# A second buffer for streamed weight rows, v weights in pieces into their place, and statistics inside the folds

## The chip, the cores and the metric

The kernel runs on one core of one Trainium2 chip, as one launch. The metric is the time of an execution in device microseconds (us). The kernel before took 717.04 us (median of three runs, 717.01 to 718.02). A core has five engines that run side by side, each with its own queue of instructions in a fixed order: TensorE (PE) multiplies matrices, VectorE (DVE), ScalarE (ACT) and GpSimd (POOL) do elementwise work, and SyncE (SP) issues the transfers (DMAs) here. They wait for each other through semaphores.

## The reference

The input x has 2048 tokens of 640 channels. Everything is float32. Cut to what matters:

```python
xn = layernorm(x)
# A: linear attention, 32 heads of 20 channels
q, k, v = split(xn @ wqkv)                      # 640 x 1920
pq, pk = per_head(q @ w_phi), per_head(k @ w_phi)
phi = lambda p: concat(softmax(p), softmax(-p))
kv, z = phi(pk).T @ v, sum(phi(pk))
A = (phi(pq) @ kv / (phi(pq) @ z + 1e-6)) @ wo  # 640 x 640
# B: MLP with its own layernorm, 1728 hidden units
B = gelu(layernorm(xn) @ w1 + b1) @ w2 + b2
return x + A + B
```

## The kernel before, in words

**Split products.** Each float32 operand is split into a high part (a rounded copy, made by ACT) and a low part (the rest, made by DVE or POOL). A product is three matmuls: high by high, high by low, low by high (`mm3`, L62 to L64). So every weight and every activation costs an ACT copy and a DVE or POOL subtraction before PE can use it.

**Blocks and chunks.** The 2048 tokens are four blocks of 512. The hidden units are 14 chunks of 128 (the last has 64). The span has three parts. In the first, to some 218 us, PE runs the MLP of blocks 0 and 1, and beside it weights and inputs for the later parts are prepared. In the second the k, v and q projections and the attention sums are made, in the third the MLP of blocks 2 and 3, and the output. The change is in the first part.

**The first part.** After a start (tokens turned, first four chunks), `cycle(g)` for g = 2 to 5 handles chunks 2g and 2g+1 for both blocks with fewer products than four (sums and differences of the halves of weights and activations, `t1` to `t4`, are multiplied). Then `mlp.passes(6, b, ...)` does chunks 12 and 13 in the plain way, for block 0 and then 1: first layer, gelu, second layer. Results leave PE through eight PSUM banks: 0 to 2 for the first layer, 3 and 4 for the folds, 5 to 7 for the second layer. The second layer's bank is added to `acc` by DVE (L311) and then free for PE again.

**Steps.** The order on PE, DVE, ACT and POOL is written out by hand. Each time PE has been given one `mm3` in a place that allows it, `next(mlp.beside)` takes one step of the work beside: `at_steps` holds (step, action) pairs, and `both` runs two such lists in step. One cycle has 38 steps. The order on SP is not written out: a scheduler places its transfers. A step is a place in the order, not a time: an engine that must wait holds everything behind it.

**What runs beside.** `weight_events` makes the operands of the next cycle from two loaded tiles of w1 (ACT L501, POOL L504, POOL L507 for sums). `second_half(j)` splits 128 rows of w2 (ACT L501, POOL L504); they come through `load_second` (SP L556) into one buffer, `r2`, so that a load is issued when the split before has read it. `prep()` has one order: `folds` multiplies weights of q and k by the head's feature map on PE (L606) and splits and stores the results; `more_stats` takes the layernorm statistics of tokens 1024 to 2047 (L129), at two of every ten steps of the folds; then `rows` turns means and scales through PE, bank 3 or 4, and sends them through DRAM; then ten tiles of y for blocks 2 and 3 are made, eight steps each: subtract on POOL (L696), multiply on DVE (L699), high part on ACT (L703), low part on DVE (L706), two stores on SP (L708). Last, five tiles of v's weights are loaded into a staging tile (L668) and split into `wkv_`. The k part of `wkv_` (product of the folds) comes back from DRAM in two loads (L824).

**At the start** POOL makes two sums of 1024 columns for `traw` (L470), and `t_events` makes differences of them on DVE (L507).

Of the kernel before, what the change touches and what calls it, by code (L numbers as in the profile page):

```python
# [15 lines left out]
P = 128  # L16
# [27 lines left out]
def tile_kernel(ctx: ExitStack, tc: tile.TileContext, x, xT, wkT, wqT, wv, wphi, wo, w1, b1, w2, b2,  # L44
# [36 lines left out]
    wq_dram = [tc.dram_tile([P, KC, F1], F32, name=f"wq{p}") for p in "hl"]  # L81
    wk_dram = [tc.dram_tile([P, KC, F1], F32, name=f"wk{p}") for p in "hl"]
# [382 lines left out]
    def next_y():  # L465
# [3 lines left out]
        for i, c in ((0, slice(0, 2)), (3, slice(2, 4))):  # L469
            nc.gpsimd.tensor_tensor(q[i], f(h[:, c]), f(l[:, c]), op=ALU.add)  # L470
# [81 lines left out]
    r2 = [None]  # L552

    def load_second(c):
        r2[0] = rp.tile([P, D], F32, name="r2")
        nc.sync.dma_start(r2[0], w2[c * P:(c + 1) * P, :])  # L556

    load_second(4)
    mlp.beside = at_steps(*t_events(), *weight_events({"11": 10, "S1": 11, "12": 12, "15": 13, "s1": 14, "s2": 15, "S3": 16, "S4": 17,
# [105 lines left out]
    def prep():  # L665
        def load_v(kc):
            raw = fp.tile([P, D], F32, name="raw")
            nc.sync.dma_start(raw, wv[kc * P:(kc + 1) * P, :])  # L668
            return raw

        def load(b, c):
# [5 lines left out]
        loads = ahead([*(lambda job=job: raws(*job) for job in jobs), *(lambda job=job: load(*job) for job in todo),  # L677
                       *(lambda kc=kc: load_v(kc) for kc in range(KC))], 1)
# [46 lines left out]
    def cycle(g, other, side):  # L725
# [30 lines left out]
        def second_half(j):  # L756
            return [hi([x for x in (w2_[j][:, 0], w2_[j][:, 1])], r2[0]), lo([w2_[j][:, 0], w2_[j][:, 1]], r2[0], nc.gpsimd)]
# [4 lines left out]
                  (3, lambda: second_half(0)[0]()), (4, lambda: second_half(0)[1]()), (5, lambda: load_second(2 * g + 1)),  # L762
                  (12, lambda: second_half(1)[0]()), (13, lambda: second_half(1)[1]())]
        if g < 5:
            events += [(14, lambda: load_second(2 * g + 2)),
                       *weight_events({"11": 3, "S1": 4, "S3": 5, "s1": 7, "s2": 10, "S4": 11, "D5": 12, "12": 15, "15": 16, "s3": 18,
                                       "22": 22, "25": 23, "s4": 27, "d5": 28}, g + 2)]
        else:
            def take(c):
                def go():  # L770
                    mlp.raw[c] = araw[c - 12], rlast[c - 12]
# [4 lines left out]
            def load_last_seconds():  # L776
                load_second(12)
                rlast.append(r2[0])
                last = rp.tile([P, KC, P], F32, name="r1").rearrange("p a b -> p (a b)")
                for o in range(0, P, 64):  # L780
                    nc.sync.dma_start(last[o:o + 64, :], w2[13 * P:F, :])
                rlast.append(last)

            rlast = []
            mlp.spare = nc.gpsimd
            events += [(14, load_last_seconds), (16, take(12)), (19, take(13)), (27, lambda: ready[12][1][1]())]
# [31 lines left out]
    mlp.beside = side  # L818
# [733 lines left out]
```

## Time and profile before

The profiled execution took 717.25 us; its span from the first to the last instruction is 715.2 us.

| engine | busy us | share |
|---|---|---|
| PE (matmul) | 703.8 | 98% |
| DVE | 501.0 | 70% |
| POOL | 438.5 | 61% |
| ACT | 353.0 | 49% |

The DMA engines moved 103.41 MB, 145 GB/s in the mean. A row of the timeline gives the start and the duration in us, the engine, the line, the operation, output<-input by the program's names (buffer numbers left out, so `r2` reads `r`), the shape, and in brackets how long the engine had been idle before it and what ended the idle time. PE's matmuls overlap, so their durations are longer than the distance between their starts.

### The profile page before, as it was taken

The page shows a single profiled execution, that of the slowest core. Times are in us where ns is not written, and L with a number is a line of the kernel's source. Part 1 is how long each engine was busy: PE and PEld are TensorE (multiplying, and loading weights), DVE is VectorE, ACT ScalarE, POOL GpSimd, SP SyncE. Part 2 cuts the span into 40 slices and gives each one's busy share as a digit, 9 for nine tenths or more (in the row PEclk, how much of TensorE's full clock was granted, in tenths as well). Part 3 has the DMA queues.
Part 4 walks back from the last instruction along what each step waited for, and adds up shares of the span by engine and source line. Part 5 has one row for each costly group of instructions (what it writes and reads, how often), then busy time and mean ns, then how long its engine had stood idle before and what let it go on. Part 6 is the DMA issues. An engine that isn't in the chain of part 4 may idle for free.

```text
span 715.2 us, 9901 instructions
## 1 busy us (share of the span) xinstructions
PE 703.8 (98%) x3368; PEld 592.6 (83%) x3368; DVE 501.0 (70%) x837; ACT 353.0 (49%) x624; POOL 438.5 (61%) x408
## 2 busy tenths in 40 slices
PE   9999999999899999999999999999999999999998
PEld 7778888877778888888888888888888888888887
DVE  7886766496643788988978887845565646778753
ACT  7744546444343454454445447556565556551310
POOL 2584433666153797797787979655677777563400
PEclk9999999999999999999999999999999999999999
DMA  9516966455763224624600705674444753163222
GB/s 331 170 40 184 286 189 191 129 176 190 239 251 147 74 78 161 152 94 178 147 1 2 183 2 187 148 217 137 131 118 130 206 148 114 42 235 121 89 75 88
DMA packets 77047, 103.41 MB, mean 145 GB/s; under 512 B 22677, under 2 KB 45861, under 8 KB 75373
## 3 DMA queue, kind: packets, MB, share of 16 engines
q1 hardware_dynamic: 76996, 102.79, 46.0%
q8 instruction: 26, 0.43, 0.3%
q14 instruction: 25, 0.20, 0.1%
HBM read 69.79 MB, written 32.97 MB: 144 GB/s over the span
## 4 chain that ended last, share of the span: by engine, by line
PE 81%; DVE 6%; issue 4%; POOL 3%; DMA 3%; ACT 2%; SPq 0%; POOLq 0%; ACTq 0%; DVEq 0%
PE bank L62 24%; PE bank L63 24%; PE bank L64 24%; PE bank L943 3%; PE bank L606 2%; PE bank L1172 1%; PE bank L1171 1%; DVE q L507 1%; POOL w L504 1%; DMA yl<-raw 1%; DVE st L129 1%; DMA raw<-in_wv 1%; POOL raw L696 1%; DVE raw L706 1%; DVE acc L311 1%
## 5 line engine op out<-in xcount | busy, mean ns | idle before, releaser
L62 PE MATMUL bank<-m,w 128*128 128x512 f32 x266 | 106.5, 400 | 5.7 <-DVE acc L311 4.6
L62 PE MATMUL bank<-y,w 128*128 128x512 f32 (+1 forms) x270 | 104.7, 388 | 0.0
L64 PE MATMUL bank<-y,w 128*128 128x512 f32 (+1 forms) x270 | 104.3, 386 | 0.0
L63 PE MATMUL bank<-y,w 128*128 128x512 f32 (+1 forms) x270 | 104.2, 386 | 0.0
L64 PE MATMUL bank<-m,w 128*128 128x512 f32 x266 | 104.2, 392 | 0.0
L63 PE MATMUL bank<-m,w 128*128 128x512 f32 x262 | 102.7, 392 | 0.0
L311 DVE TENSOR_TENSOR acc<-bank,acc 128x512 f32<-128x512 f32 x120 | 80.7, 680 | 22.8 <-PE bank L64 18.4
L62 PE MATMUL bank<-wkh,y 128*128 128x512 f32 (+2 forms) x240 | 87.6, 365 | 0.0
L63 PE MATMUL bank<-wkl,y 128*128 128x512 f32 (+2 forms) x240 | 87.1, 363 | 0.0
L64 PE MATMUL bank<-wkh,y 128*128 128x512 f32 (+2 forms) x240 | 86.9, 362 | 0.0
L889 ACT ACTIVATE m<-bank 128x512 f32<-128x512 f32 (+1 forms) x64 | 26.5, 440 | 83.6 <-PE bank L64 60.2
L908 POOL TENSOR_TENSOR m<-m,mx 128x640 f32<-128x640 f32 (+2 forms) x48 | 44.4, 938 | 35.9 <-DVE mx L896 35.9
L62 PEld LDWEIGHTS bank<-m,w 128*128 128x128 f32 x266 | 50.3, 189 | 19.3 <-DVE acc L311 7.7
L1165 POOL TENSOR_TENSOR e<-e,m 128x512 fp32r<-128x512 f32 (+1 forms) x28 | 40.0, 1432 | 38.5 <-ACT m L1164 21.4
L64 PEld LDWEIGHTS bank<-y,w 128*128 128x128 f32 x270 | 50.7, 188 | 10.3
L64 PEld LDWEIGHTS bank<-m,w 128*128 128x128 f32 x266 | 50.3, 189 | 10.7
L62 PEld LDWEIGHTS bank<-y,w 128*128 128x128 f32 x270 | 50.7, 188 | 10.1
L63 PEld LDWEIGHTS bank<-y,w 128*128 128x128 f32 x270 | 50.7, 188 | 10.1
L915 DVE TENSOR_REDUCE sm<-m 128x64 f32<-128x1280 f32 x32 | 47.3, 1479 | 15.8 <-ACT m L913 15.6
L63 PEld LDWEIGHTS bank<-m,w 128*128 128x128 f32 x262 | 49.7, 190 | 9.7 <-DVE m L754 0.2
L913 ACT ACTIVATE m<-m,rs_all 128x1280 f32<-128x1280 f32 x32 | 43.8, 1368 | 21.8 <-POOL m L908 21.7
L56 POOL TENSOR_TENSOR w<-r,w 128x640 fp32r<-128x640 f32 x31 | 49.0, 1600 | 7.8 <-ACT w L53 7.7
(260 smaller groups left out, 1635.4 us busy)
## 6 DMA issues: line engine op xcount, KB each, us to landing
r<-in_w SPq DMA_DIRECT2D x43, 320.0 KB
e<-e SPq DMA_DIRECT2D x40, 256.0 KB
e<-acc SPq DMA_DIRECT2D x52, 160.0 KB
acc<-in_xT SPq DMA_DIRECT2D x4, 1280.0 KB
a<-in_w SPq DMA_DIRECT2D x9, 320.0 KB
xb<-in_x SPq DMA_DIRECT2D x8, 320.0 KB
xs<-in_x SPq DMA_DIRECT2D x8, 320.0 KB
raw<-in_xT SPq DMA_DIRECT2D x10, 256.0 KB
```

Of the source, the lines that this page charges most:

```text
L56: eng.tensor_tensor(lo, src, f(hi), op=ALU.subtract)
L62: nc.tensor.matmul(ps, lh, rh, start=first, stop=False, **kw)
L63: nc.tensor.matmul(ps, lh, rl, start=False, stop=False, **kw)
L64: nc.tensor.matmul(ps, ll, rh, start=False, stop=last, **kw)
L311: nc.vector.tensor_tensor(acc[b][:, m, :], pw, acc[b][:, m, :], op=ALU.add)
L606: nc.tensor.matmul(ps[:, c + i * kd:c + (i + 1) * kd], raw[n, g][:, (kc + i) * P:(kc + i + 1) * P], wpt[:, g, :kd // DF, 1:], start=True, ...
L889: return nc.scalar.activation(p3[:, :, c], ps.rearrange("p (h f) -> p h f", h=H), AF.Copy).ins
L908: subs[n, t] = nc.gpsimd.tensor_tensor(ep[:, s], a, b, op=ALU.subtract)
L913: exps[n, t] = nc.scalar.activation(e, e, AF.Exp, scale=rs_all[:, t:t + 1])
L915: nc.vector.tensor_reduce(sm, e.rearrange("p s (h f) -> p (s h) f", f=DH), axis=AX, op=ALU.add)
L943: nc.tensor.matmul(kvp[g // 2][:P, (g % 2) * 240:(g % 2) * 240 + 240].rearrange("p (s f) -> p s f", s=4), v[:, g * VS:g * VS + P], ft[:, : ...
L1165: nc.gpsimd.tensor_tensor(pl, e, f(ph), op=ALU.subtract)
```

## The change

- `load_second` gets two buffers, `r2` for even chunks and `r1` for odd ones, each loaded again after its own split has been read. Two loads are issued before the first cycle. Chunks 12 and 13 use the same two; the separate load of the last rows goes, and their split moves: chunk 12's from the last cycle into the last chunk pair, beside chunk 13's.
- v's weights are first copied inside DRAM to `wv_dram` (five transfers, at the beginning), then loaded in five pieces straight into the low part of `wkv_`, and split there in place, within `last_weights`; the staging loads at the end of `prep` go. The k weights come in ten pieces instead of two loads.
- The statistics are taken at three of every ten steps of the folds, and `rows` follows them there instead of after the folds. So the y tiles begin four steps earlier.
- POOL's two sums of 1024 columns become four of 512, and the first sum of weights (S1) moves from step 11 to 11.5.

```diff
-        for i, c in ((0, slice(0, 2)), (3, slice(2, 4))):
-            nc.gpsimd.tensor_tensor(q[i], f(h[:, c]), f(l[:, c]), op=ALU.add)
+        for c in range(4):
+            nc.gpsimd.tensor_tensor(q[c // 2 * 3][:, c % 2], f(h[:, c]), f(l[:, c]), op=ALU.add)
...
     def load_second(c):
-        r2[0] = rp.tile([P, D], F32, name="r2")
-        nc.sync.dma_start(r2[0], w2[c * P:(c + 1) * P, :])
+        r2[c % 2] = rp.tile([P, KC, P], F32, name=f"r{2 - c % 2}").rearrange("p a b -> p (a b)")
+        n = min(P, F - c * P)
+        for o in range(0, P, n):
+            nc.sync.dma_start(r2[c % 2][o:o + n, :], w2[c * P:c * P + n, :])
 
     load_second(4)
+    load_second(5)
+    copies = [(12 + 5 * kc, lambda kc=kc: nc.sync.dma_start(wv_dram[:, kc], wv[kc * P:(kc + 1) * P, :])) for kc in range(KC)]
...
-        loads = ahead([*(lambda job=job: raws(*job) for job in jobs), *(lambda job=job: load(*job) for job in todo),
-                       *(lambda kc=kc: load_v(kc) for kc in range(KC))], 1)
+        loads = ahead([*(lambda job=job: raws(*job) for job in jobs), *(lambda job=job: load(*job) for job in todo)], 1)
...
-        more = more_stats()
+        more = chain(more_stats(), rows(fp, mlp.px))
         for i, _ in enumerate(folds(loads)):
-            if i % 10 in (5, 8):
+            if i % 10 in (5, 7, 9):
                 next(more, None)
             yield
         fs.close()
         finish(more)
-        yield from rows(fp, mlp.px)
...
-        for kc in range(KC):
-            raw = next(loads)
-            for _ in range(3):
-                yield
-            split(*[w[:, kc, F1 + 2 * F2:] for w in wkv_], raw, eng=nc.gpsimd)
...
-                  (3, lambda: second_half(0)[0]()), (4, lambda: second_half(0)[1]()), (5, lambda: load_second(2 * g + 1)),
-                  (12, lambda: second_half(1)[0]()), (13, lambda: second_half(1)[1]())]
+                  (3, lambda: second_half(0)[0]()), (4, lambda: second_half(0)[1]()), (5, lambda: load_second(2 * g + 2)),
+                  (12, lambda: second_half(1)[0]()), (13, lambda: second_half(1)[1]()), (14, lambda: load_second(2 * g + 3))]
...
-            events += [(14, load_last_seconds), (16, take(12)), (19, take(13)), (27, lambda: ready[12][1][1]())]
+            events += [(16, take(12)), (19, take(13))]
...
-    for p in range(2):
-        nc.sync.dma_start(f(wkv_[p][:, :, :F1]), wk_dram[p])
+    def last_weights():
+        events = []
+        for kc in range(KC):
+            k, v = slice(0, F1), slice(F1 + 2 * F2, CB[2])
+            raw = f(wkv_[1][:, kc, v])
+            events += [(2 * kc, lambda kc=kc, raw=raw: nc.sync.dma_start(raw, wv_dram[:, kc])),
+                       (2 * kc + 7, lambda kc=kc, raw=raw: split(wkv_[0][:, kc, v], wkv_[1][:, kc, v], raw, eng=nc.gpsimd)),
+                       *((2 * kc + 10 + p, lambda kc=kc, p=p: nc.sync.dma_start(f(wkv_[p][:, kc, k]), wk_dram[p][:, kc])) for p in range(2))]
+        return at_steps(*events)
+    mlp.beside = both(last_weights(), side)
...
         if b == 0:
-            ready[13][1][1]()
+            for c in (12, 13):
+                ready[c][1][1]()
```

The diff tells little of where the scheduler puts SP's transfers, and of what stands behind what on POOL. On SP, at the end of the last cycle, before (`yh`, `yl` are y's stores, `raw<-in_xT` the loads of its tiles, `wkh` and `wkl` the two parts of `wkv_`, `in_wv` v's weights):

```order
L708 DMA yl_76<-raw 128x512
L673 DMA raw<-in_xT 128x512
L824 DMA wkh<-wkh 128x5x512
L824 DMA wkl<-wkl 128x5x512
L708 DMA yh_75<-xs 128x512
L708 DMA yl_76<-raw 128x512
```

and in the change, from the same store of y on:

```order
L706 DMA yl_76<-raw 128x512
L812 DMA wkl<-wv__79 128x640 x3
L673 DMA raw<-in_xT 128x512
L812 DMA wkl<-wv__79 128x640 x2
L814 DMA wkh<-wkh 128x512
L814 DMA wkl<-wkl 128x512
L814 DMA wkh<-wkh 128x512
L706 DMA yh_75<-xs 128x512
L814 DMA wkl<-wkl 128x512
L706 DMA yl_76<-raw 128x512
```

The v pieces now stand ahead of the k weights, and the last stores of y stand between the k pieces; before, v's loads came after them, at the end. On POOL, in the last chunk pair, before (`m<-m` of 64 rows is the low half of chunk 13's hidden units, L290, once for each block; `w` is the weight tile, `v` the tile of values):

```order
L290 TENSOR_TENSOR m_1948<-m_1921,m_1948 64x512
L243 MEMSET w_189 64x640
L244 TENSOR_TENSOR w_189<-r_1767,w_189 64x640
L56 TENSOR_TENSOR wkl<-raw,wkh 128x640 x3
L290 TENSOR_TENSOR m_2051<-m_2022,m_2051 64x512
L56 TENSOR_TENSOR wkl<-raw,wkh 128x640 x2
L861 MEMSET v_2165 128x1408
L861 MEMSET v_2168 128x1408
```

and in the change:

```order
L291 TENSOR_TENSOR m_1956<-m_1929,m_1956 64x512
L56 TENSOR_TENSOR w_189<-r_1735,w_189 128x640
L244 MEMSET w_190 64x640
L245 TENSOR_TENSOR w_190<-r_1783,w_190 64x640
L56 TENSOR_TENSOR wkl<-wkl,wkh 128x640 x4
L855 MEMSET v_2176 128x1408
L855 MEMSET v_2179 128x1408
L56 TENSOR_TENSOR wkl<-wkl,wkh 128x640
L291 TENSOR_TENSOR m_2066<-m_2038,m_2066 64x512
```

The second `m<-m` now stands behind all five splits of v, the split of chunk 12's rows of w2 and the two memsets; before, only three splits stood ahead of it.

More of the change, by code (lines that the diff above doesn't have):

```diff
@@ L1 @@
 from contextlib import ExitStack
-from itertools import zip_longest
+from itertools import chain, zip_longest
 import concourse.bass as bass
@@ L665, in prep @@
     def prep():
[L666 to L669, printed above, removed]
         def load(b, c):
@@ L756, in second_half @@
         def second_half(j):
-            return [hi([x for x in (w2_[j][:, 0], w2_[j][:, 1])], r2[0]), lo([w2_[j][:, 0], w2_[j][:, 1]], r2[0], nc.gpsimd)]
+            t = [w2_[j][:, 0], w2_[j][:, 1]]
+            return [hi(t, r2[j]), lo(t, r2[j], nc.gpsimd)]
         events = [(2, copy(za, "a")), (9, copy(zb, "a")), (14, total(za, "c")), (16, copy(zc, "a")), (16.5, total(zc, "d")),
@@ L770, in go @@
                 def go():
-                    mlp.raw[c] = araw[c - 12], rlast[c - 12]
+                    mlp.raw[c] = araw[c - 12], r2[c - 12]
                     ready[c] = mlp.take_parts(c, mlp.tiles[c % 4])
@@ L774, in take @@
                 return go
[L776 to L784, printed above, removed]
             mlp.spare = nc.gpsimd
-            events += [(14, load_last_seconds), (16, take(12)), (19, take(13)), (27, lambda: ready[12][1][1]())]
+            events += [(16, take(12)), (19, take(13))]
         mlp.beside = both(at_steps(*((when - 1, what) for when, what in events)), side)
```

11 lines of the change are left out of this document (5 added, 6 removed).

## The prediction

> **What bounds the kernel now.** I read the busy time of each engine first, then TensorE (PE) in stretches, then PE's rows at each place where its pace breaks, and last, for each such place, the rows of the engine that PE waited for.
>
> ```profile
> PE 703.8 (98%) x3368; PEld 592.6 (83%) x3368; DVE 501.0 (70%) x837; ACT 353.0 (49%) x624; POOL 438.5 (61%) x408
> ```
>
> PE is busy for 98% of the span, so a change that removes no matmul can win only the places where PE stands. The next view gives PE busy by stretch, with granted clock, DMA share and GB/s in the last three columns.
>
> ```profile
> 180.00:190.00 10.00, 8.77 (x32) 7.12 (x33) 7.44 (x12) 2.51 (x4) 0.03 (x1) 0.83 0.86 296
> 260.00:460.00 200.00, 200.00 (x1048) 174.98 (x1047) 168.30 (x253) 104.75 (x160) 166.15 (x167) 1.00 0.38 110
> ```
>
> From 260 to 460 PE never stands; in the ten microseconds after 180 it does. PE's own rows (start, duration, what; in brackets the idle time) show each place:
>
> ```profile
> 34.52 0.49 PE L62 MATMUL bank<-m,w 128*128 128x512 f32 x1 [1.04 <-DVE acc L309]
> 47.65 0.50 PE L62 MATMUL bank<-m,w 128*128 128x512 f32 x1 [0.35 <-DVE acc L311]
> 151.03 0.50 PE L62 MATMUL bank<-m,w 128*128 128x512 f32 x1 [0.31 <-DVE acc L311]
> 169.15 0.50 PE L62 MATMUL bank<-th,w 128*128 128x512 f32 x1 [0.95 <-ACT m L740]
> 178.45 0.39 PE L63 MATMUL bank<-m,w 128*128 128x512 f32 x1
> 178.68 0.39 PE L64 MATMUL bank<-m,w 128*128 128x512 f32 x1
> 181.23 0.80 PE L62 MATMUL bank<-m,w 128*128 128x512 f32 x1 [2.16 <-DVE acc L311]
> 184.70 0.39 PE L64 MATMUL bank<-m,w 128*128 128x512 f32 x1
> 187.00 0.39 PE L62 MATMUL bank<-y,w 128*128 128x512 f32 x1
> 210.44 0.50 PE L62 MATMUL bank<-m,w 128*128 128x512 f32 x1 [1.74 <-DVE acc L311]
> 213.52 0.39 PE L306 MATMUL bank<-m,w 128*128 128x512 f32 x1
> 218.50 0.39 PE L62 MATMUL bank<-wkh,y 128*128 128x512 f32 x1
> ```
>
> A matmul of 512 columns lasts 0.39 us but the next starts 0.23 us after it (178.45 to 178.68), so each bracketed idle time costs 0.16 us more than it says. The losses are 1.2 (at 34.52), 0.5 (47.65), 0.5 (151.03), 1.1 (169.15, call it A), 2.3 (181.23, call it B) and 1.9 us (210.44, call it C). B has a second part: from 181.23 to 184.70 are eight starts in 3.47 us where 1.82 would do, at a granted clock of 0.83 over the stretch, so B costs 2.3 + 1.6 = 3.9. Together 9.1 us stand to be won, and nothing more without taking out matmuls.
>
> The Trainium skill ("TensorE: Matmul & The Clock Gate", section "What's actually happening") puts the slow state after an idle window of about 3.4 us; here the clock sank after an idle time of 2.16 us, and not after 1.74. By the page's number the 1.6 us would not hang on B's gap and B would be worth 2.3; I go by the rows.
>
> **The change part by part.** A. The buffer for rows of w2 is single: on the queue of SyncE (SP) its load stands behind y's stores, and ScalarE (ACT) waits for it.
>
> ```profile
> 163.12 0.41 SPq L556 DMA_DIRECT2D r<-in_w  x1
> 167.36 0.74 ACT L501 ACTIVATE w<-r 128x640 fp32r<-128x640 f32 x1 [4.58 <-DMA r<-in_w]
> 168.52 0.58 ACT L740 ACTIVATE m<-bank 128x512 f32<-128x512 f32 x1
> 168.17 1.54 POOL L504 TENSOR_TENSOR w<-r,w 128x640 fp32r<-128x640 f32 x1 [6.25 <-ACT w L501]
> ```
>
> ACT stands 4.58 us at L501, the bank copy L740 queues behind it, and PE behind L740. With two buffers this load is issued a cycle earlier (some 26 us), as soon as GpSimd (POOL) has read the buffer's former rows. That removes all of A, 1.1 us. What is late next on ACT is nothing: the other operand of L740 is PE's own bank.
>
> B. The same wait holds POOL idle for 6.25 us, and the work that it should have done then collides with VectorE (DVE) later:
>
> ```profile
> 173.44 1.35 DVE L699 TENSOR_TENSOR raw<-raw,t 128x512 f32<-128x512 f32 x1 [1.19 <-POOL raw L696]
> 176.83 2.06 DVE L706 TENSOR_TENSOR raw<-raw,xs 128x512 fp32r<-128x512 f32 x1
> 179.42 1.16 DVE L699 TENSOR_TENSOR raw<-raw,t 128x512 f32<-128x512 f32 x1
> 182.29 0.68 DVE L706 TENSOR_TENSOR raw<-raw,xs 128x512 fp32r<-128x512 f32 x1
> 180.50 1.27 DVE L311 TENSOR_TENSOR acc<-bank,acc 128x512 f32<-128x512 f32 x2
> 176.32 2.02 POOL L56 TENSOR_TENSOR w<-r,w 128x640 fp32r<-128x640 f32 x1
> ```
>
> DVE stands 1.19 us for POOL, then L699, L706 and L699 take 1.35, 2.06 and 1.16 while POOL works, against 0.68 when it doesn't: 1.19 + 0.67 + 1.38 + 0.48 = 3.7 us of delay in front of the L311 that frees PE's bank. I follow the new order with these durations: the split of chunk 11 runs on POOL at some 163 instead of 168.2, one split (2.02 us) leaves this stretch for the next stage, and the y preparation starts four steps earlier, which puts L706 where L699 was. Then POOL is up to date at 171 and each L311 is done over 1 us before PE asks for its bank again. I take all of B, 3.9; the bounds are 0 (the collisions only move) and 3.9. The same shift is what I expect at 151.03: 0.5, bounds 0 and 0.5.
>
> C. The v weights' load blocks ACT (6.45 us), and with it the gelu on which DVE's L311 hangs.
>
> ```profile
> 206.25 0.74 ACT L53 ACTIVATE wkh<-raw 128x640 fp32r<-128x640 f32 x1 [6.45 <-DMA raw<-in_wv]
> 195.73 1.29 POOL L290 TENSOR_TENSOR m<-m,m 64x512 fp32r<-64x512 f32 x1 [3.73 <-issue]
> 196.97 0.63 POOL L243 MEMSET w<- 64x640 f32 x1
> 197.68 1.58 POOL L244 TENSOR_TENSOR w<-r,w 64x640 fp32r<-64x640 f32 x1
> 199.22 3.08 POOL L56 TENSOR_TENSOR wkl<-raw,wkh 128x640 fp32r<-128x640 f32 x2
> 215.74 2.49 POOL L861 MEMSET v<- 128x1408 f32 x2
> ```
>
> Now five pieces go straight into wkl, once PE and POOL have left that space (some 170 to 173), and land by about 178, well before ACT's first split. C as such is gone: 1.9. But it gives some back. Count from the start of the last chunk pair, t0 = 187.00 before. POOL's first L290 starts at t0 + 8.73. Behind it now stand, in one row, w2's split for chunk 12 (1.55, as L504 above), the memset (0.63) and L244 (1.58), four v splits (4 x 1.54), the two memsets of v (2.49, in front now, behind before), the fifth split (1.54) and only then the second L290 (1.29). Sum: 8.73 + 1.29 + 1.55 + 0.63 + 1.58 + 6.16 + 2.49 + 1.54 + 1.29 = 25.26; less 0.06 us of overlap at each border, some 24.9. PE, without C, comes to the L306 that reads this result at 213.52 - 187.00 - 1.9 = t0 + 24.6, and needs it a signal earlier. I take a new wait of 0.7 us (bounds 0 and 1.9). So C brings 1.2.
>
> Start. POOL's two sums of 1024 columns become four of 512, and the first sum of weights (S1) is put behind the first low half.
>
> ```profile
> 27.11 5.21 POOL L470 TENSOR_TENSOR q<-y,y 128x1024 f32<-128x1024 f32 x2
> 31.24 1.63 DVE L261 TENSOR_TENSOR m<-m,m 128x512 fp32r<-128x512 f32 x1
> 39.59 3.98 DVE L507 TENSOR_TENSOR q<-q,q 128x1024 f32<-128x1024 f32 x2 [1.63 <-POOL q L178]
> 40.77 1.73 POOL L507 TENSOR_TENSOR sraw<-a 128x256 f32<-128x256 f32 x1
> 46.92 0.68 DVE L311 TENSOR_TENSOR acc<-bank,acc 128x512 f32<-128x512 f32 x1
> ```
>
> L261 ends (32.87) half a microsecond after POOL's second sum (32.32): it waited for that instruction to end. With pieces of 1.3 us it ends some 1.3 us sooner, which pays the 1.2 at 34.52. PE then comes earlier to 47.65, but DVE there is set by POOL's chain (L507 starts when POOL's last sum is there), which the pieces don't shorten. What shortens it is S1: at 40.77 it collides with the second L507, and now waits for ACT. I take 0.6 to 0.9 off the L311 at 46.92, so the two stalls together bring 0.8 (bounds 0 and 1.7).
>
> Costs that I set near nothing. Two rows, the statistics of one tile's halves and the copy of the turned rows:
>
> ```profile
> L129 DVE BATCH_NORM_STATS2 st<-xs x16: 441/476/484, 70.8 to 100.0; 128x6 f32<-128x320 f32 x16
> 129.63 0.28 DVE L191 COPY sr<-bank 16x128 f32<-16x128 f32 x1
> ```
>
> The statistics come three to ten steps instead of two, one tile (2 x 0.48 and a small aggregate, 1.1 us) more in each of the first periods of ten steps (each step three matmuls, 0.68 us, and the folds' own); DVE has that room there, since the dense run of L311 comes only after step 28, where statistics stood before and stand no more. The turn of the rows through PE takes bank 3 one step before a fold uses it; the copy that frees it (0.28) stands behind one add of 0.68, so PE may wait 0 to 0.7; I take 0.15. The five copies of v inside DRAM (1.6 MB) are issued behind the last large load:
>
> ```profile
> 8.00:12.00 4.00, 3.97 (x30) 3.41 (x29) 3.79 (x15) 3.83 (x9) 1.56 (x1) 1.00 1.04 406
> 24.00:28.00 4.00, 4.00 (x21) 3.32 (x20) 2.00 (x9) 3.84 (x7) 1.03 (x2) 1.00 0.72 192
> ```
>
> The DMA engines are full at first (share 1.04) and done within the stretch that ends at 28 (0.72). At 390 GB/s the copies take 4.2 us, and 8.4 if reading and writing count apart; only the w1 rows of the next chunks stand behind them, due at 40.77 on POOL. Nothing is lost unless they take 14 us.
>
> Sum: 0.8 + 0.5 + 1.1 + 3.9 + 1.2 - 0.15 = 7.35; I keep 0.15 back for small waits not foreseen and say 7.2. The profiled execution took 717.25 us (span 715.2), 0.2 above the median 717.04; so 710.05 for an execution like it, **709.8 as a median**.
>
> **Rivals.** (1) B stays: DVE has as many instructions in that cycle as before, and the stretched ones may only meet POOL elsewhere. For it: DVE and POOL are 70% and 61% busy. Against it: POOL's 6.25 us of idle time are used. Then 717.04 - 7.2 + 3.9 = 713.7. (2) No wait comes in place of those removed, and the start brings everything: 717.04 - 9.1 = 707.9. Against it: the row of POOL work counted above. (3) Slower: the pieces don't overlap. Ten pieces of k (262 KB) and five of v (328 KB), 4.26 MB, stand where two loads of 1.3 MB stood, each needed whole at the projection, which comes at t0 + 31.5 less C, 209.9 on the new clock (t0 about 180.3). If each took the 4.2 us from issue to ACT's start that the load at 163.12 took, one behind the other, 15 pieces from 171 on would end at 234 and the projection would wait 24 us: 734. It decides at 4.26 MB in 39 us, 109 GB/s; below 92 the kernel is slower than before. Against it: the first loads, of 328 KB each, ran at 406 GB/s together. The Trainium skill ("DMA: Bandwidth & Descriptors", section "Measured (HBM→SBUF, 128 partitions, SWDGE, issued from GpSimd)") advises batches of at least 1 MiB, against this split; its fit of 2.0 us plus the bytes at 436 GB/s for each, one after another, would end at about 211 and cost some 1 us; it is measured on another queue than SP's, and the 406 GB/s here speaks against it. (4) The change doesn't do what it says: something else on the queues of ACT and SP holds the same stalls, within 1 us of before: 716.5.
>
> **How the numbers follow.** Forecast 0.61 (708.6 to 711.5 by its bounds on C and the start), (1) 0.15, (2) 0.11, (3) 0.05, (4) 0.08. A measurement of this kernel tells 0.2%, 1.4 us, from no change. Faster: 0.61 + 0.15 + 0.11 = 0.87; same 0.08; slower 0.05. The range runs from (2) to just past (1), 707.5 to 714.3.
>
> **What would show it.** Right: no idle time of ACT on loads of r or of v; PE without a gap from 120 to 200 and clock 1.00 in every slice; one gap of under a microsecond at the second L306 (now L307), released by POOL; the first gap near 34 gone and that near 47 longer. Wrong: a gap of over 1 us released by L311 in the cycle before the last chunk pair (then rival 1), a wait of PE for wkh or wkl at the first projection (rival 3), or a PE wait for a bank in the folds (then the statistics cost what I set at nothing).

## The result, and the profile after

The change takes 713.12 us (median of three runs, 712.67 to 713.58) against 717.04: the ratio is 0.9941, 95% interval 0.9918 to 0.9964. It is faster, by 3.9 us, and by 4.6 between the two profiled executions (717.25 to 712.67; spans 715.2 to 710.9). The prediction said 7.2 and 709.8. The time lies inside its range, next to the time of its first rival, but not for that rival's reason: what that rival expected to stay went away, and the missing 3 us lie elsewhere. Three profiled executions of the experiments below (`e3_y_later`, `e9_one_buffer_split_back` and `e11_before_split_late`) ran at a far lower pace throughout (spans of 1183.5, 1429.0 and 1429.0 us), so their gaps can't be read and they are left out of the times below.

The busy times of the change, and its window from 180 to 190 us (granted clock, DMA share and GB/s at the end):

```profile
PE 701.1 (99%) x3368; PEld 591.7 (83%) x3368; DVE 502.6 (71%) x837; ACT 353.0 (50%) x624; POOL 439.7 (62%) x410
```

```profile
180.00:190.00 10.00, 10.00 (x46) 8.28 (x45) 6.43 (x10) 3.18 (x5) 1.43 (x1) 1.00 1.03 393
```

In the stretch where PE was busy for 8.77 of 10 us at a clock of 0.83 it is now busy throughout at 1.00. PE's own rows in the change, at the places that the prediction named (each bracket again costs 0.16 us more than it says), and at three landmarks:

```profile
33.50 0.50 PE L62 MATMUL bank<-m,w 128*128 128x512 f32 x1 [0.28 <-DVE acc L310]
47.56 0.50 PE L62 MATMUL bank<-m,w 128*128 128x512 f32 x1 [1.27 <-DVE acc L312]
149.82 0.50 PE L63 MATMUL bank<-m,w 128*128 128x512 f32 x1 [1.30 <-DVE m L746]
153.74 0.50 PE L62 MATMUL bank<-m,w 128*128 128x512 f32 x1 [0.42 <-DVE acc L312]
168.83 0.39 PE L62 MATMUL bank<-th,w 128*128 128x512 f32 x1
178.74 0.50 PE L62 MATMUL bank<-m,w 128*128 128x512 f32 x1 [0.23 <-DVE acc L312]
182.95 0.39 PE L62 MATMUL bank<-y,w 128*128 128x512 f32 x1
208.95 0.50 PE L307 MATMUL bank<-m,w 128*128 128x512 f32 x1 [1.35 <-POOL m L291]
214.07 0.39 PE L62 MATMUL bank<-wkh,y 128*128 128x512 f32 x1
```

The same matmuls stood at 47.65, 169.15, 187.00 and 218.50 before. So the change leads by 0.1 us at the end of the start, by 0.3 behind place A, by 4.05 at the beginning of the last chunk pair and by 4.4 at the projection. Place by place:

| place | predicted gain | measured gain |
|---|---|---|
| start (34 and 47 us) | 0.8 | 0.1 |
| 47 us to A | 0.5 | -0.9: two new gaps, 1.46 + 0.58, instead of 0.5; slips under 0.25 us elsewhere give some back |
| A (169 us) | 1.1 | 1.1 |
| B (181 us) | 3.9 | 3.7 |
| C and what takes its place (last pair) | 1.2 | 0.4 (the new wait is 1.5, not 0.7) |

The loads behave as predicted. ACT's splits of streamed rows (L502) and its copies of the bank (L732) no longer wait for a transfer:

```profile
164.08 0.72 ACT L502 ACTIVATE w<-r 128x640 fp32r<-128x640 f32 x1
167.67 0.60 ACT L732 ACTIVATE m<-bank 128x512 f32<-128x512 f32 x1 [2.87 <-PE bank L64]
```

There is no wait of PE for `wkh` or `wkl` either: all 15 pieces overlap, at 393 GB/s in the window above, and the rival in which they cost time is refuted.

### The profile page after: what moved, and what is told of

Read it like the earlier page. It is cut to its first block, busy times and chain, and to the rows that moved or that the text cites. A ratio compares the mean times of both kernels' runs of the same rounds, so it can differ in the third digit from the quotient of the medians.

```text
span 710.9 us, 9918 instructions
## 1 busy us (share of the span) xinstructions
PE 701.1 (99%) x3368; PEld 591.7 (83%) x3368; DVE 502.6 (71%) x837; ACT 353.0 (50%) x624; POOL 439.7 (62%) x410
## 4 chain that ended last, share of the span: by engine, by line
PE 84%; DVE 5%; POOL 5%; issue 3%; ACT 1%; DMA 1%; POOLq 0%; ACTq 0%; DVEq 0%
PE bank L62 25%; PE bank L63 25%; PE bank L64 25%; PE bank L937 3%; PE bank L611 2%; PE bank L1166 1%; PE bank L1165 1%; POOL w L56 1%; DVE st L130 1%; DVE q L508 1%; POOL raw L694 1%; DVE raw L697 1%; POOL wkl L56 1%; POOL w L505 1%; POOL sraw L508 1%
## 5 line engine op out<-in xcount | busy, mean ns | idle before, releaser
L312 DVE TENSOR_TENSOR acc<-bank,acc 128x512 f32<-128x512 f32 x120 | 80.7, 681 | 21.9 <-PE bank L64 16.4
L56 POOL TENSOR_TENSOR w<-r,w 128x640 fp32r<-128x640 f32 x31 | 48.6, 1589 | 8.0 <-ACT w L53 7.9
```

The costliest lines, as they stand in the source:

```text
L56: eng.tensor_tensor(lo, src, f(hi), op=ALU.subtract)
L312: nc.vector.tensor_tensor(acc[b][:, m, :], pw, acc[b][:, m, :], op=ALU.add)
```

## Where the missing gain went

**The start.** POOL and DVE in the change:

```profile
27.05 5.96 POOL L471 TENSOR_TENSOR q<-y,y 128x512 f32<-128x512 f32 x4
38.53 2.54 POOL L179 TENSOR_TENSOR q<-y,y 128x512 f32<-128x512 f32 x2
28.18 0.71 DVE L56 TENSOR_TENSOR m<-m,m 128x512 fp32r<-128x512 f32 x1 [1.50 <-ACT m L53]
30.08 1.78 DVE L262 TENSOR_TENSOR m<-m,m 128x512 fp32r<-128x512 f32 x1
39.84 3.64 DVE L508 TENSOR_TENSOR q<-q,q 128x1024 f32<-128x1024 f32 x2 [2.89 <-POOL q L179]
44.00 2.90 DVE L508 TENSOR_TENSOR q<-q,q 128x1024 f32<-128x1024 f32 x2
46.83 0.68 DVE L312 TENSOR_TENSOR acc<-bank,acc 128x512 f32<-128x512 f32 x1
```

The four shorter sums let DVE in between, and the gap at 34 us went from 1.04 to 0.28. But the L312 on which PE waits next ends where it did: it starts at 46.83 (46.92 before). It stands behind four differences L508, and these start when POOL has made the first of its last two sums (L179, 38.53). The four sums L471 ahead in POOL's queue take 5.96 us instead of 5.21, and the differences start at 39.84, 0.25 later than before; the first two then take 3.64 instead of 3.98, and the two effects nearly cancel. PE came earlier and waited longer.

**At 150 us.** VectorE before (two rows), then GpSimd and VectorE in the change:

```profile
143.46 1.21 DVE L699 TENSOR_TENSOR raw<-raw,t 128x512 f32<-128x512 f32 x1 [2.26 <-POOL raw L696]
145.19 1.05 DVE L754 TENSOR_TENSOR m<-m,m 128x512 fp32r<-128x512 f32 x1
```

```profile
145.11 1.30 POOL L694 TENSOR_TENSOR raw<-raw,t 128x512 f32<-128x512 f32 x1
146.45 1.21 DVE L697 TENSOR_TENSOR raw<-raw,t 128x512 f32<-128x512 f32 x1 [2.31 <-POOL raw L694]
147.58 0.68 DVE L312 TENSOR_TENSOR acc<-bank,acc 128x512 f32<-128x512 f32 x1
148.18 1.58 DVE L746 TENSOR_TENSOR m<-m,m 128x512 fp32r<-128x512 f32 x1
```

Four steps earlier, a y tile's L697 stands in another place among DVE's instructions. It waits 2.31 us for POOL, and behind it in DVE's queue stand an add L312 and the low half L746 that PE's next matmul reads. The same wait was there before (2.26 us for a tile at 143.46), and a low half (L754) stood behind it too, but PE had no gap over 0.25 us there.

**In the last chunk pair.** GpSimd in the change:

```profile
191.69 1.30 POOL L291 TENSOR_TENSOR m<-m,m 64x512 fp32r<-64x512 f32 x1 [10.04 <-ACT m L290]
196.94 6.65 POOL L56 TENSOR_TENSOR wkl<-wkl,wkh 128x640 fp32r<-128x640 f32 x4
203.53 2.48 POOL L855 MEMSET v<- 128x1408 f32 x2
205.98 1.58 POOL L56 TENSOR_TENSOR wkl<-wkl,wkh 128x640 fp32r<-128x640 f32 x1
207.64 1.26 POOL L291 TENSOR_TENSOR m<-m,m 64x512 fp32r<-64x512 f32 x1
```

This is the row that the prediction counted. The first L291 starts 8.74 us behind 182.95 (forecast 8.73), PE comes when forecast, but the second L291 ends 25.95 behind it, not 24.9: the four splits took 6.65 instead of 6.16 (a subtraction of VectorE's, L56 at 200.46 for 1.69 us, ran in that time), and there was no overlap at the borders.

## The experiments

All times are medians; ratios are to the kernel before on the same chip. `e2_stats_old` to `e5_v_split_late` ran together on one chip, without the change itself. There the kernel before took 718.45 us, and the run to compare the others with is `e4_one_buffer`, which has the change's gaps: against its 712.83, `e2_stats_old` gains 1.05, `e3_y_later` 1.55 and `e5_v_split_late` 1.62. The runs from `e6_one_buffer_stats_old` on, `e0_change` and `e1_start_old` ran on another chip.

| run | us | ratio | 95% |
|---|---|---|---|
| change | 713.12 | 0.9941 | 0.9918 to 0.9964 |
| `e0_change`, the change again | 713.40 | 0.9955 | 0.9940 to 0.9971 |
| `e1_start_old` | 713.16 | 0.9950 | 0.9933 to 0.9966 |
| `e2_stats_old` | 711.78 | 0.9918 | 0.9897 to 0.9938 |
| `e3_y_later` | 711.28 | 0.9911 | 0.9890 to 0.9932 |
| `e4_one_buffer` | 712.83 | 0.9933 | 0.9915 to 0.9950 |
| `e5_v_split_late` | 711.21 | 0.9910 | 0.9893 to 0.9927 |
| `e6_one_buffer_stats_old` | 713.67 | 0.9958 | 0.9946 to 0.9970 |
| `e7_both_orders` | 710.21 | 0.9910 | 0.9895 to 0.9924 |
| `e8_start_diff_late` | 708.98 | 0.9894 | 0.9879 to 0.9908 |
| `e9_one_buffer_split_back` | 713.68 | 0.9963 | 0.9947 to 0.9979 |
| `e10_split_back` | 711.93 | 0.9925 | 0.9895 to 0.9954 |
| `e11_before_split_late` | 720.04 | 1.0054 | 1.0039 to 1.0069 |

### Is it the second buffer? (`e4_one_buffer`, `e6_one_buffer_stats_old`)

```diff
-        r2[c % 2] = rp.tile([P, KC, P], F32, name=f"r{2 - c % 2}").rearrange("p a b -> p (a b)")
+        r2[c % 2] = rp.tile([P, KC, P], F32, name="r1" if c == 13 else "r2").rearrange("p a b -> p (a b)")
...
     load_second(4)
-    load_second(5)
...
-                  ... (5, lambda: load_second(2 * g + 2)),
+                  ... (5, lambda: load_second(2 * g + 1)),
-                  ... (14, lambda: load_second(2 * g + 3))]
+                  ... (14, lambda: load_second(2 * g + 2)), (14.5, lambda: g < 5 or load_second(13))]
```

> The change with one buffer for w2's rows again (every load of an even or odd chunk goes to the same buffer, chunk 13 alone keeps its own); the v pieces, the statistics and the start stay as changed. Theory: the two buffers carry both A and B, because the wait for the load makes POOL late and only that makes DVE late. Then ACT waits over 4 us for the load in the last cycle again, PE stands again at A (1.1 us) and B (2 to 4 us with the slow clock), and the time is 3 to 5 us above the change's 713.1: 716 to 718. Rival: B was ended by the y tiles that come four steps earlier; then only A returns, 714 to 714.5, with clock 1.00 throughout.

Measured: 712.83 us, and the same five gaps as the change. Neither expectation came true: with one buffer A and B stayed away. SyncE, ScalarE and TensorE in that kernel:

```profile
161.59 0.33 SPq L559 DMA_DIRECT2D r<-in_w  x1
164.57 0.74 ACT L502 ACTIVATE w<-r 128x640 fp32r<-128x640 f32 x1 [0.35 <-DMA r<-in_w]
178.77 0.50 PE L62 MATMUL bank<-m,w 128*128 128x512 f32 x1 [0.24 <-DVE acc L312]
```

The row load is issued at 161.59 and waited for only 0.35 us. In the kernel before it was issued at 163.12, behind a load of x and two stores of y on the same queue, and waited for 4.58. What may have put it ahead is the statistics' edit: it moves the y tiles, and so y's loads and stores, against the row loads (all on SP's queue). Putting the statistics back as well tests that:

```diff
-        more = chain(more_stats(), rows(fp, mlp.px))
+        more = more_stats()
-            if i % 10 in (5, 7, 9):
+            if i % 10 in (5, 8):
...
         finish(more)
+        yield from rows(fp, mlp.px)
```

> One buffer for w2's rows and the statistics at their old place together; the v pieces and the start as changed. Either alone left A and B out. Theory: A and B hang on where the scheduler puts the load of chunk 11 on SP: behind a load of y's tiles that waits for an earlier store, or ahead of it. Two buffers make that place harmless, four steps' shift of the y tiles changes the place. In this kernel the load stands behind the load of a y tile and one store again, so ACT waits for it over 2 us, and A and B return: gaps of about 0.9 and 2 us near 166 and 178, 716 to 718. Rival: A and B were a chance of the old timing (what the start or the v pieces moved ended them); then they stay out and the time is that of the old statistics with two buffers, 711.8.

Measured: 713.67 us. SyncE, ScalarE, TensorE, VectorE and GpSimd in it:

```profile
162.82 0.41 SPq L559 DMA_DIRECT2D r<-in_w  x1
167.10 0.74 ACT L502 ACTIVATE w<-r 128x640 fp32r<-128x640 f32 x1 [4.39 <-DMA r<-in_w]
168.90 0.50 PE L62 MATMUL bank<-th,w 128*128 128x512 f32 x1 [0.77 <-ACT m L732]
176.57 0.68 DVE L704 TENSOR_TENSOR raw<-raw,xs 128x512 fp32r<-128x512 f32 x1
177.78 0.68 DVE L697 TENSOR_TENSOR raw<-raw,t 128x512 f32<-128x512 f32 x1
178.06 1.54 POOL L694 TENSOR_TENSOR raw<-raw,t 128x512 f32<-128x512 f32 x1 [1.96 <-DMA raw<-in_xT]
179.11 0.50 PE L62 MATMUL bank<-m,w 128*128 128x512 f32 x1 [0.31 <-DVE acc L312]
```

A is back, nearly whole: the load is late again, ACT waits 4.39 us, PE 0.77 (0.95 before). So A needs both the single buffer and the old order on SP, and either part of the change alone removes it (`e2_stats_old`, below, has the old order with two buffers, and no gap there). B is not back. ACT's wait, from which the prediction derived B, is there, yet DVE's L704 and L697 take 0.68 each, where they took 2.06 and 1.16 before. (179.11 is the same matmul as 181.23 before and 178.74 in the change, the 18th ahead of the last chunk pair.)

### What was B? (`e10_split_back`, `e9_one_buffer_split_back`, `e11_before_split_late`)

What still differs from before on POOL at this place is the split of chunk 12's rows of w2 (2.02 us at 176.32 before), which the change moved into the last chunk pair. In `e6_one_buffer_stats_old` POOL stands idle there for 1.96 us, its instructions on both sides are those of before, and VectorE's rows run 0.26 us ahead of before up to L704, the first that the split met. The next edit puts it back; `e10_split_back` is the change with it, `e9_one_buffer_split_back` is `e6_one_buffer_stats_old` with it.

```diff
-            events += [(16, take(12)), (19, take(13))]
+            events += [(16, take(12)), (19, take(13)), (27, lambda: ready[12][1][1]())]
...
-            for c in (12, 13):
-                ready[c][1][1]()
+            ready[13][1][1]()
```

> The change (two buffers, statistics within the folds) with chunk 12's second split alone put back on GpSimd in the last cycle (step 27). Theory (the split holds VectorE there whatever the buffers do): with VectorE earlier than before by the wait for the load that is gone, it slips by about 1.3 us, the gap at 178.7 us grows from 0.2 to about 1.5 and stays too short for a slow clock; the gap at 209 goes by 1.35; 713.2 us, the same as the change. Rival (what stalled TensorE at 181 us was the wait for the load): the gap at 178.7 stays as it is and only that at 209 goes; 712.0 us.

Measured: 711.93 us, the rival's time, and a gap of the theory's size, but at another matmul. ScalarE, GpSimd, VectorE and TensorE in `e10_split_back`, then TensorE in `e0_change`, which is the change run again:

```profile
177.31 0.72 ACT L53 ACTIVATE w<-r 128x640 fp32r<-128x640 f32 x1
178.11 1.58 POOL L56 TENSOR_TENSOR w<-r,w 128x640 fp32r<-128x640 f32 x1 [2.10 <-DMA wkl<-wv__79]
179.65 3.00 POOL L694 TENSOR_TENSOR raw<-raw,t 128x512 f32<-128x512 f32 x2
181.43 1.78 DVE L697 TENSOR_TENSOR raw<-raw,t 128x512 f32<-128x512 f32 x1 [1.18 <-POOL raw L694]
183.86 0.50 PE L62 MATMUL bank<-m,w 128*128 128x512 f32 x1 [1.50 <-DVE acc L312]
```

```profile
182.15 0.50 PE L62 MATMUL bank<-m,w 128*128 128x512 f32 x1 [0.49 <-DVE acc L312]
```

With nothing else changed, a gap of 1.50 stands six matmuls ahead of the last chunk pair: POOL's subtraction for a y tile stands behind the split, DVE's L697 waits for it and then takes 1.78, and the adds behind are late. This is not the place of B: the matmul on which PE stood at 181.23 before, and at 178.74 in the change, is the 18th ahead of the pair, and it has no gap here. At the matmul of 183.86 the change's profile has no gap, but that of `e0_change` has one of 0.49, without the split. So of the 1.50, the split accounts for some 1.0 to 1.5. No load holds it: the profile names one of v's at the end of POOL's idle time, but the high part from ACT, which this split reads, ended at 178.03, 0.08 us ahead of its start. The profiled execution took 713.43 us, with 1.1 us lost at the start that the change's didn't lose; the other three took 711.2 to 712.1. The gap at 209 is gone (POOL's row is shorter by that split). So the split alone can make a gap of B's kind in this stretch, without a wait for a load; the lower times of the other three executions leave it open whether the gap is there in each.

> The change with one buffer for the second-layer rows, the statistics where they were, and chunk 12's second split put back on GpSimd in the last cycle (step 27), where the kernel before had it. Beside the same kernel without that put back (713.67 us). Theory (the stall at 181 us came from that split: it holds VectorE's L699 and L706, and behind them the add on which TensorE waits): the gap comes back at 179 to 182 us with 1.5 to 2.5 us and some matmuls behind it at a slow clock, about 3.4 more; GpSimd's row of splits ahead of the second L291 is 1.55 shorter, which takes the 1.35 gap at 209 down to about nothing; 715.8 us. Rival (the split has nothing to do with it): the gap at 179 stays at 0.3 to 0.5 and only the gap at 209 goes; 712.3 us.

Measured: 713.68 us, but the nine executions fall into two groups, five from 713.1 to 713.7 and four from 715.4 to 716.2, the upper one where the theory put it. The granted clock on record with each of them parts them the same way: its mean is 1.000 in all five of the lower group and 0.998 in all four of the upper one. In `e6_one_buffer_stats_old`, without the split, it is 0.999 or 1.000 in all seven. So the split brings the slow clock back, in some executions; that it does so through the gap at B's matmul is argued, since no gaps can be read in this run.

The kernel before has the same two groups. Of its 33 executions on this chip, 14 have a mean clock of 0.999 or 1.000 and a median of 715.6 us, and 19 have 0.995 to 0.998 and a median of 717.3. The second part of B, 1.6 us of slow clock, is thus a matter of the execution: the profiled one had it (mean clock 0.998), and some two in five did not.

The last run moves the split alone, in the kernel before:

```diff
-            events += [(14, load_last_seconds), (16, take(12)), (19, take(13)), (27, lambda: ready[12][1][1]())]
+            events += [(14, load_last_seconds), (16, take(12)), (19, take(13))]
...
-            ready[13][1][1]()
+            for c in (12, 13):
+                ready[c][1][1]()
```

> The kernel before with one edit: chunk 12's second split leaves the last cycle (step 27) and stands with chunk 13's at the head of the last chunk pair, as in the change. Buffers, loads, statistics and v are as before, so ScalarE's wait for the row load ahead of it (4.58 us, loss A) stays. Theory (loss B hangs on that split, not on the load): the gap at 181 us falls from 2.16 to 0.2 to 0.5 and no matmul behind it runs at a slow clock, about 3.4 less; A's gap at 169 and C's at 210 stay, and the split has room on GpSimd in the last pair (idle 3.73 ahead of its first L290); 713.6 us against 717.0. Rival (B came from GpSimd's wait for the load, as was predicted): the gap at 181 stays at about 2.2 and the time at 717.0.

Measured: 720.04 us, slower than before by 0.5%, which neither expected. The edit changed the order of SP's transfers as well. SyncE in `e11_before_split_late`, where only the order is to be read:

```profile
380.89 0.32 SPq L854 DMA_DIRECT2D w<-wql  x1
381.30 0.48 SPq L668 DMA_DIRECT2D raw<-in_wv  x1
```

A load of q's weights (1.3 MB) now stands ahead of the first of the last three v loads; before, that place had a load of 0.33 MB (`r<-in_wo`, issued ahead of `raw<-in_wv` because its buffer was free). v's loads are what C waits for. At the 390 GB/s that the prediction used, the megabyte in front is worth some 2.5 us more of C, before any slow clock. That estimate would make most of the loss of 3.5 if B had stayed, and not the 7 that would have to be lost if B had gone. Each of the five executions has a mean clock of 0.995, lower than the 0.998 of the profiled execution before, so TensorE ran slow for longer than there; where, no row shows. So whether B went away in this kernel is not known. What is shown of B is therefore this: ACT's wait for the load does not make it (`e6_one_buffer_stats_old`); where the split is missing, VectorE is not held and the clock stays up (the same run), and with the split back the clock sinks again in some executions (`e9_one_buffer_split_back`). That moving the split is all there is to it is not shown.

### The order of the y tiles (`e2_stats_old`, `e3_y_later`)

`e2_stats_old` is the change with the statistics' edit undone (the diff shown for `e6_one_buffer_stats_old`, two buffers kept); `e3_y_later` keeps the statistics inside the folds and only lets the y tiles begin where they did before:

```diff
-        for _ in range(6):
+        for _ in range(10):
             yield
```

> The change with the statistics and the turn of the rows as before (two of ten steps, rows after the folds), so that the y tiles start at their old step; two buffers, v pieces and the start stay as changed. Theory: the two gaps of the change near 150 and 154 (1.46 and 0.57 us more than the pace) come from the y tiles' steps: a DVE multiply that waits for POOL now stands right ahead of the low half that PE needs first. Then they shrink to the 0.5 to 0.8 of before and the time is about 1.3 us under the change's: 711.8. Rival: they come from POOL's fuller order with two buffers, whatever the y tiles' step; then they stay, 713.1.

> The change with four more empty steps ahead of the first y tile; the statistics stay inside the folds. Theory: it is the steps of the y tiles and not the place of the statistics that makes the gaps near 150 and 154; they shrink as with the old statistics, and both kernels have the same time within 0.5 us: 711.8. Rival: the statistics inside the folds matter; the gaps stay or another stands near 105 to 115.

Measured: 711.78 and 711.28 us, both near the theory. In `e2_stats_old` the gaps at 149.82 and 153.74 are gone and one of 0.34 at 151.04 is there, as before the change. It has lost something new on the way. GpSimd, VectorE and TensorE in it:

```profile
195.80 7.68 POOL L56 TENSOR_TENSOR wkl<-wkl,wkh 128x640 fp32r<-128x640 f32 x5
199.32 4.70 DVE L56 TENSOR_TENSOR m<-m,m 128x512 fp32r<-128x512 f32 x1 [3.48 <-ACT m L53]
205.27 0.50 PE L62 MATMUL bank<-m,w 128*128 128x512 f32 x1 [1.77 <-DVE acc L312]
```

A subtraction that takes 0.68 alone took 4.70 us beside POOL's row of splits. `e3_y_later` shows by its time that the statistics inside the folds cost nothing by themselves: the four steps that they let the y tiles move forward did the damage. The gaps of `e7_both_orders`, below, which has the same edit, show it too: near 150 us only one of 0.37 is left.

### The row on GpSimd (`e5_v_split_late`)

```diff
-                       (2 * kc + 7, lambda kc=kc, raw=raw: split(...
+                       (2 * kc + (7 if kc < 3 else 15), lambda kc=kc, raw=raw: split(...
```

> The change with the last two of the five v splits eight steps later, so that on POOL only three stand ahead of the second low half of chunk 13 (L291), as before the change. Theory: the gap of 1.35 us near 209 is POOL's row of work ahead of that instruction; two splits less (3.1 us) end it, and the time is 1.5 us under the change's: 711.6. Rival: PE there waits for something that comes at the same time (the last loads or ACT); then a gap of at least 0.8 us stays or goes to the first projection, 712.5 to 713.1.

Measured: 711.21 us, as the theory said. GpSimd in `e5_v_split_late`:

```profile
197.12 4.63 POOL L56 TENSOR_TENSOR wkl<-wkl,wkh 128x640 fp32r<-128x640 f32 x3
204.46 1.29 POOL L291 TENSOR_TENSOR m<-m,m 64x512 fp32r<-64x512 f32 x1
205.82 3.11 POOL L56 TENSOR_TENSOR wkl<-wkl,wkh 128x640 fp32r<-128x640 f32 x2
```

With two v splits behind the second L291 instead of ahead, it ends at 205.75 instead of 208.90, PE doesn't wait for it, and the projection doesn't wait for the later splits either. So the whole 1.9 of C was to be had.

### The start (`e1_start_old`)

```diff
-        for c in range(4):
-            nc.gpsimd.tensor_tensor(q[c // 2 * 3][:, c % 2], f(h[:, c]), f(l[:, c]), op=ALU.add)
+        for i, c in ((0, slice(0, 2)), (3, slice(2, 4))):
+            nc.gpsimd.tensor_tensor(q[i], f(h[:, c]), f(l[:, c]), op=ALU.add)
...
-    ... weight_events({"11": 10, "S1": 11.5, ...
+    ... weight_events({"11": 10, "S1": 11, ...
```

> The change with the two edits at the start undone (the conv sums as two of 1024 columns, and chunk 3's split on GpSimd at step 11 again). Theory (the stall at the start only moved, from 34 to 47 us: GpSimd's sums and VectorE's four differences set when the add ahead of the second chunk pair ends, in either order): gaps of about 1.0 at 34 us and 0.3 at 47 us as in the kernel before, and the same time as the change, 713.1 us within 0.3. Rival (the edits are worth the 0.8 that was predicted): 713.9 us.

Measured: 713.16 us, the theory's. TensorE in `e1_start_old`:

```profile
34.42 0.50 PE L62 MATMUL bank<-m,w 128*128 128x512 f32 x1 [1.04 <-DVE acc L310]
47.57 0.50 PE L62 MATMUL bank<-m,w 128*128 128x512 f32 x1 [0.35 <-DVE acc L312]
```

The old gaps are back, and the matmul at 47.57 starts within 0.01 us of where it does in the change (47.56). The two edits at the start are worth nothing by themselves.

### A version that beats both (`e0_change`, `e7_both_orders`, `e8_start_diff_late`)

> The change itself once more, beside the others on one chip, as their measure. Every theory: 712.7 to 713.6, and the same five gaps of PE (near 34, 48, 150, 154 and 209).

Measured: 713.40 us, with the gaps of the change and three more in the profiled execution (0.59 at 7.84, 0.49 at 182.15, 0.45 at 471.71), so gaps of half a microsecond come and go between executions of one kernel. It is the measure for the two below, which ran on the same chip. `e7_both_orders` has the edits of `e3_y_later` and `e5_v_split_late` together.

> The change with two edits at once: four more empty steps ahead of the first y tile, and the last two v splits behind the second low half of chunk 13. Theory: the two are independent, 1.5 us each: the gaps near 150, 154 and 209 are gone but for 0.5, and the wait of DVE for POOL's five splits in a row (4.7 us for one subtraction, seen with the old statistics) is short, since only three stand in a row: 709.5 to 710. Rival: the y tiles, now later, meet the v splits, and a gap near 205 takes the place: 711.

Measured: 710.21 us, just above the theory's range. Its large gap left is that of the start:

```profile
47.66 0.50 PE L62 MATMUL bank<-m,w 128*128 128x512 f32 x1 [1.26 <-DVE acc L312]
```

`e8_start_diff_late` takes two of the four differences L508 out from ahead of the adds:

```diff
-... (5, add(v, q2, q2, ALU.subtract, q1)), (7, add(v, q4, q4, ALU.subtract, q2))
+... (13, add(v, q2, q2, ALU.subtract, q1)), (15, add(v, q4, q4, ALU.subtract, q2))
```

> As the kernel with both orders, and in the start DVE's third and fourth difference (L508, 2.9 us together) stand behind the first and second addition that frees a bank (L312) instead of ahead of it. Theory: the gap of 1.27 us near 47.5 is DVE's own order: the addition that PE waits for stands behind two differences that nobody needs for 15 us. It goes but for 0.3, and the kernel is 1.1 us faster than with both orders: 708.5 to 709. Rival: POOL's sums set that time, or the differences are soon missed by ACT and PE; then the gap moves on and the time stays within 0.4 us.

Measured: 708.98 us (708.59 to 709.40), 4.4 below the change on the same chip. VectorE in it:

```profile
44.00 0.69 DVE L312 TENSOR_TENSOR acc<-bank,acc 128x512 f32<-128x512 f32 x1
45.20 1.77 DVE L508 TENSOR_TENSOR q<-q,q 128x1024 f32<-128x1024 f32 x1
```

The add that started at 46.83 starts at 44.00, and the gap at 47 us is gone; what is left from there on is one gap of 0.37, with 0.92 and 0.33 ahead of it (at 7.92 and 33.52). With this third edit the start brings a gain, 1.2 from `e7_both_orders` to here, where 0.8 had been predicted for the change.

## Why the prediction was right and wrong

- **What bounds the kernel: right.** All of the difference lies in the places where PE stood before, and in the new ones; elsewhere the two kernels' matmuls drift by no more than 0.5 us in any stretch.
- **A, 1.1: right in size, too narrow in cause.** Step "with two buffers this load is issued a cycle earlier": true, but `e4_one_buffer` shows that the moved y tiles alone would have freed the load as well, and `e6_one_buffer_stats_old` that it comes late only if neither is there.
- **B, 3.9: near in size (3.7), wrong in cause.** The step "The same wait holds POOL idle for 6.25 us, and the work that it should have done then collides with VectorE (DVE) later" failed: with ACT's wait back (4.39 us), the collision stayed away. A later sentence, "one split (2.02 us) leaves this stretch for the next stage", named what counts by `e6_one_buffer_stats_old`; the prediction gave it a side part. That the size came out so near is in part luck: the change moved that split as well. And 1.6 of the 3.9 is slow clock (0.50 from 182 to 184 us in the profiled execution; the 0.83 is a mean over ten microseconds) that some two in five executions of the kernel before don't have. The result does not bear out the first rival (B stays), whose time it nearly has.
- **151.03, 0.5: wrong sign.** "The same shift is what I expect at 151.03" failed. The four steps that the y tiles moved forward put DVE's wait for POOL (2.31 us) ahead of the low half that PE reads: 2.0 us of gaps instead of 0.5. The lower bound "0" left no room for a loss; the prediction had not followed what stands behind L697 in the new order at this place. `e2_stats_old` shows it by its gaps, `e3_y_later` by its time.
- **C, 1.9 less a new wait: the mechanism and its place were right, a term was mis-sized.** The new wait at the second L307 is 1.5, inside its bounds of 0 to 1.9, instead of 0.7: the term "four v splits" took 6.65, not 6.16, and the overlap of 0.06 at each border was not there. (The rows before don't show it at every border either: the memset ends at 197.60 and L244 starts at 197.68. And 0.06 at eight borders would give 24.8, not 24.9.)
- **The start, 0.8: inside its bounds of 0 to 1.7 at the lower end, 0.1.** The step "I take 0.6 to 0.9 off the L311 at 46.92" failed: it now starts at 46.83. With S1 out of their way the first two differences do take 0.34 us less. But the prediction saw that DVE there "is set by POOL's chain", and took that chain as unchanged; the change makes its sums longer (5.96 against 5.21) and the differences start 0.25 later. `e1_start_old` shows a gain of 0.0.
- **Costs set near nothing: right** for the statistics' own time, the copies of v in DRAM and the pieces; the cost was in the order, not in the work.
- **The chances:** faster was right. That the range held the time is luck: it reached to the first rival, which did not come about, and the likeliest case's own range (708.6 to 711.5) missed it by 1.6 us. It took no bound below zero for the place at 151, where the loss was.

## What to carry to other kernels

When an edit gives a group of beside-work an earlier place, look in the new order at what stands behind each of its waits on the in-order engine, and not at the average room; here four steps cost some 1.5 us, and moving only that group back returned them. A gap removed at the head of a chain whose end is set by another engine only moves: follow the chain to the row that releases the next wait before booking a gain. And a row of work counted instruction by instruction predicts a new wait's place well; book the border between instructions at zero, not as overlap.

## What the runs showed of the hardware

- DVE's subtraction of 512 columns with both inputs in SBUF, 0.68 us alone, took 4.70 us in `e2_stats_old` when it came up 3.5 us into a row of five GpSimd splits (7.68 us in all); it ended 0.5 us after the row did. The Trainium skill ("SBUF — State Buffer", section "SBUF: two separate sides") says that the engine that comes second blocks until the other's instruction is through; here VectorE was held through what was left of three instructions, one behind the other. In the change it got in after the first of four sums (L56 at 28.18, 0.71 us). The runs don't show what decides between the two.
- PE's granted clock was 0.50 from 182 to 184 us in the profiled execution before, right behind an idle time of 2.16 us, and it did not sink after 1.77 us in `e2_stats_old`, where the next matmuls but the first start 0.23 us apart. Of 33 executions of the kernel before on one chip, 14 have a mean clock of 0.999 or 1.000; whether their gap was as long is not known.
- While the 15 pieces of 0.26 and 0.33 MB, issued one by one, were under way, 393 GB/s moved (180 to 190 us, stores of y included); the loads at the beginning of the kernel before came to 406.
